# Loading k and q by head, turning them in program order, and holding six chunks at a change of batch

## The chip, the cores and the metric

The kernel runs on one core of a Trainium2 chip. Its time is the device time of one execution in microseconds (us); lower is better. Three executions of the kernel before took 1262.25, 1262.31 and 1267.04 us, so the median is 1262.31 us. Engines are named as in the profile: PE is the matrix engine (PEld its weight loads), DVE the vector engine, ACT the scalar engine, POOL is GpSimd, SP the engine whose queue issues nearly all transfers (SPq).

## The reference

All inputs are float32 or float64 (the mixer's weights); the output is float32. The shapes are 8 batches, 8 heads, 576 tokens, 64 channels a head, 128 features. With `phi` for the features:

```python
def phi(x):
    proj = einsum('bhsd,df->bhsf', x, w_phi)
    proj = proj - max(abs(proj), axis=-1, keepdims=True)
    return concatenate([exp(proj), exp(-proj)], axis=-1)
q_p, k_p = phi(q), phi(k)
kv  = einsum('bhsf,bhsd->bhfd', k_p, v)
z   = sum(k_p, axis=2)
x   = einsum('bhsf,bhfd->bhsd', q_p, kv) / (einsum('bhsf,bhf->bhs', q_p, z)[..., None] + 1e-6)
x   = x as (batch, token, 8 * 64)
u   = x + (xT @ U @ V)T           # xT: tokens last; U is 576 x 32, V is 32 x 576
out = u + max(u @ w_ch1, 0) @ w_ch2   # 512 -> 2048 -> 512
```

So there are two parts: linear attention for each pair of batch and head, and a mixer over the tokens and channels of each batch.

## The kernel before

**Tiles and stages.** Of a batch's 576 tokens 512 (SM) are worked on as four tiles of 128 (NT = 4), and the last 64 (ST, the tail) apart: tails of two batches share a tile `xt`, and the tails of all batches make up a ninth group of mixer rows. Attention goes by pairs of heads (class `Pair`), four pairs a batch, 32 in all. The mixer goes by groups of 512 rows (class `Mixer`): the 8 batches, and then the tails.

**A pair.** k and q of two heads are loaded into a tile `raw` (tag "raw", two buffers, so k and q of one pair at a time). From batch 2 on (`self.split`) they are loaded in blocks of 32 x 32 so that one DVE instruction, `nc.vector.transpose` (L321, the *turn*), makes them channel by token in place. Then ACT and DVE split them into a high and a low part `T` (L324, L325), PE projects them (`pk` L470, `pq` L496), and ACT, DVE and POOL (an all-reduce over partitions) make the features. `kt` and `kv` are the sums over the tokens of k's features with v; DVE adds them up in `kv` (L407, L408, L411). `xp` (L555) is the product of q's features with `kv`, which `normalize` (L534) divides into the batch's token tile `x`; `xpt` (L542) is the same for the tail, into `xt`.

**The token stage** (class `Tokens`, function `tokens`), at the end of each batch: `x` is split (`xs`, L633, L634), multiplied with U (`pp`, L647), then with V for each of the four tiles and the tail (`vp`, L663; below `vp_0` to `vp_4`), added to `x` (L664) and stored to memory (`u_dram<-x`, L665). From there 16 transfers bring it back in blocks (`y<-u_dram`, L691), DVE turns it (L697), and ACT and DVE split it into `uT_hi` and `uT_lo` (L249, L250).

**The mixer's chunks.** A group's work is 32 chunks of 12 matmuls: 16 `hidden` (`ph`, L705, then the relu into `h_hi` L710 and `h_lo` L711) and 16 `add` (`o`, L726, onto four banks `o_0` to `o_3`). The chunks of one batch are mixed between the steps of the next batch's attention: the list `todo`, emptied by `mix`, at the pace of `Pace`. At the end of a batch `mix(len(todo) - HELD)` leaves `HELD` chunks of the old group for the time until the new group's `uT` is there. After an old group's last chunk, `finish` adds its banks onto rows that were loaded again (`st`, L745) and stores them (L746); the group of tails adds them onto `x_tail` (L749) and stores that (L755), and this ends the kernel.

**What sets the order.** The code is written in program order, but a scheduler orders each engine's instructions by a model of their times before the program is built. An instruction on which `tc.keep_in_program_order` is called stays behind whatever the code traced last on its engine. At run time each engine works in its built order, and a wait of one instruction holds all behind it on that engine. `keep_busy` adds small matmuls (`busy`) where no chunks are to be had.

## Time and profile before

| what | value |
|---|---|
| median of 3 runs | 1262.31 us (1262.25 to 1267.04) |
| profiled execution | 1269.13 us, its span 1267.3 us |
| mean granted clock of PE | 0.956 |
| PE, PEld busy | 1216.5 us (96%), 1032.7 us (81%) |
| DVE, ACT, POOL busy | 865.7, 622.1, 315.5 us |
| chain that ended last | 69% PE, 14% DVE, 5% SPq, 5% ACT |

The profile is of one execution. Its page gives busy times, a strip of 40 slices of the span with busy tenths and the clock that PE was granted, and the costliest groups of instructions. Matmuls are pipelined, so a busy PE is not a PE at its best: how many matmuls a stretch holds and the granted clock say more. Views by stretch give each engine's busy time and the clock between two points of time; timelines give single instructions with the idle time before them and what ended it.

### The profile page before, as it was taken

The page shows a single profiled execution, that of the slowest core. Times are in us where ns is not written, and L with a number is a line of the kernel's source. Part 1 is how long each engine was busy: PE and PEld are TensorE (multiplying, and loading weights), DVE is VectorE, ACT ScalarE, POOL GpSimd, SP SyncE. Part 2 cuts the span into 40 slices and gives each one's busy share as a digit, 9 for nine tenths or more (in the row PEclk, how much of TensorE's full clock was granted, in tenths as well). Part 3 has the DMA queues.
Part 4 walks back from the last instruction along what each step waited for, and adds up shares of the span by engine and source line. Part 5 has one row for each costly group of instructions (what it writes and reads, how often), then busy time and mean ns, then how long its engine had stood idle before and what let it go on. Part 6 is the DMA issues. An engine that isn't in the chain of part 4 may idle for free.

```text
span 1267.3 us, 18400 instructions
## 1 busy us (share of the span) xinstructions
PE 1216.5 (96%) x6331; PEld 1032.7 (81%) x6333; DVE 865.7 (68%) x1781; ACT 622.1 (49%) x1271; POOL 315.5 (25%) x202
## 2 busy tenths in 40 slices
PE   8999998999997999999999999899998999999997
PEld 7878887878886888888887888688887888788886
DVE  5857879877789767888789868876788663412211
ACT  6857687535554555555555455444555541111110
POOL 3433434321322213223232323132223230000000
PEclk9979998989996999989998999889998999999999
DMA  4767222332326332453336223633245114811311
GB/s 134 244 232 239 72 70 62 86 91 75 77 71 150 79 78 63 135 117 76 82 103 146 65 74 83 150 84 79 62 117 129 42 51 139 197 67 50 100 67 33
DMA packets 268893, 129.03 MB, mean 102 GB/s; under 512 B 228944, under 2 KB 241536, under 8 KB 268800
## 3 DMA queue, kind: packets, MB, share of 16 engines
q1 hardware_dynamic: 268800, 127.86, 37.1%
q8 instruction: 50, 0.82, 0.3%
q14 instruction: 43, 0.35, 0.1%
HBM read 103.63 MB, written 24.17 MB: 101 GB/s over the span
## 4 chain that ended last, share of the span: by engine, by line
PE 69%; DVE 14%; SPq 5%; ACT 5%; DMA 4%; issue 3%; POOL 1%; DVEq 0%; ACTq 0%; POOLq 0%
PE ph L705 25%; PE o L726 25%; PE xp L555 7%; PE kt L387 3%; SPq L271 2%; SPq L691 2%; DVE T L325 2%; PE pk L470 2%; DVE w L242 2%; DMA y<-u_dram 1%; PE pp L647 1%; PE xpt L542 1%; DMA u_dram<-x 1%; ACT w_ab L138 1%; PE kv_ps L516 1%
## 5 line engine op out<-in xcount | busy, mean ns | idle before, releaser
L705 PE MATMUL ph<-uT_hi,w 128*128 128x512 f32 x1152 | 392.2, 401 | 1.9 <-DVE h_lo L711 1.2
L726 PE MATMUL o<-w,h_hi 128*128 128x512 f32 x1152 | 315.4, 398 | 3.8 <-ACT h_hi L710 3.6
L705 PEld LDWEIGHTS ph<-uT_hi,w 128*128 128x128 f32 x1152 | 221.0, 193 | 47.0 <-DVE h_lo L711 1.7
L726 PEld LDWEIGHTS o<-w,h_hi 128*128 128x128 f32 x1152 | 213.5, 190 | 49.3 <-ACT h_hi L710 6.7
L705 PE MATMUL ph<-uT_lo,w 128*128 128x512 f32 x576 | 230.3, 400 | 4.4 <-DVE uT_lo L250 4.3
L711 DVE SCALAR_TENSOR_TENSOR h_lo<-ph,h_hi 128x512 fp32r<-128x512 f32 x144 | 98.8, 687 | 171.8 <-ACT h_hi L710 170.6
L358 POOL PARTITION_ALL_REDUCE zs<-zs x48 | 106.6, 2221 | 414.0 <-DVE zs L357 373.6
L710 ACT ACTIVATE h_hi<-ph 128x512 fp32r<-128x512 f32 x144 | 85.9, 597 | 242.7 <-PE ph L705 231.6
L726 PE MATMUL o<-w,h_lo 128*128 128x512 f32 x576 | 183.6, 394 | 0.0
L434 POOL PARTITION_ALL_REDUCE qp<-qp x64 | 132.6, 2073 | 152.6 <-ACT qp L433 152.4
L555 PEld LDWEIGHTS xp<-kv,qp 128*128 128x128 f32 x1024 | 135.8, 210 | 4.8 <-ACT qp L436 0.7
L555 PE MATMUL xp<-kv,qp 128*128 128x65 f32 x1024 | 137.3, 292 | 0.5 <-DVE kp_t L421 0.3
L705 PEld LDWEIGHTS ph<-uT_lo,w 128*128 128x128 f32 x576 | 111.0, 193 | 29.8 <-DVE uT_lo L250 8.0
L726 PEld LDWEIGHTS o<-w,h_lo 128*128 128x128 f32 x576 | 105.3, 188 | 19.2
L325 DVE TENSOR_TENSOR T<-raw,T 64x512 fp32r<-64x512 f32 x96 | 77.0, 802 | 13.8 <-ACT T L324 11.0
L424 ACT ACTIVATE kp<-kp 128x512 f32<-128x512 f32 x64 | 40.5, 632 | 84.1 <-DVE kp L421 50.9
L436 ACT ACTIVATE qp<-qp 128x512 f32<-128x512 f32 x64 | 40.3, 630 | 53.3 <-DVE qp L435 52.9
L324 ACT CAST T<-raw 64x512 fp32r<-64x512 f32 x96 | 59.3, 618 | 14.5 <-PE pq L496 12.7
L146 POOL INT64_ADD w_ab<-w_ab x32 | 44.3, 1384 | 79.7 <-DVE w_ab L142 48.9
L372 DVE TENSOR_TENSOR klo<-kp,khi 128x1024 fp32r<-128x1024 f32 x48 | 60.9, 1268 | 2.5 <-PE kt L387 2.2
L473 ACT COPY kp<-pk 128x256 f32<-128x256 f32 x96 | 34.3, 371 | 52.4 <-PE pk L470 52.0
L321 DVE STREAM_TRANSPOSE raw<-raw 128x512 f32<-128x512 f32 x48 | 34.0, 709 | 37.9 <-DMA raw<-in_q_dram 21.0
(146 smaller groups left out, 1836.5 us busy)
## 6 DMA issues: line engine op xcount, KB each, us to landing
w<-kept SPq DMA_DIRECT2D x78, 512.0 KB
words<-in_moe_w_ch_dram SPq DMA_DIRECT2D x32, 512.0 KB
vb<-in_v_dram SPq DMA_DIRECT2D x64, 128.0 KB
u_dram<-x SPq DMA_DIRECT2D x32, 256.0 KB
st<-u_dram SPq DMA_DIRECT2D x16, 512.0 KB
out_dram<-st SPq DMA_DIRECT2D x32, 256.0 KB
y<-u_dram SPq DMA_DIRECT2D x112, 64.0 KB
raw<-in_k_dram SPq DMA_DIRECT2D x192, 32.0 KB
```

Of the source, the lines that this page charges most:

```text
L146: nc.gpsimd.int64_add(a64, a64, b64)
L324: nc.scalar.copy(out=m[here, s, :], in_=x_[here])
L325: nc.vector.tensor_sub(m[there, s, :], x_[here], f32(m[here, s, :]))
L358: nc.gpsimd.partition_all_reduce(zs[:, 1, :], zs[:, 0, :], P, ReduceOp.add)
L372: nc.vector.tensor_sub(lo, kp, f32(hi))
L424: nc.scalar.activation(out=kp[:, :, 0:F], in_=kp[:, :, F:2 * F], func=AF.Exp)
L434: nc.gpsimd.partition_all_reduce(qp[:, 0, :], qp[:, 1, :], P, ReduceOp.absmax)
L555: nc.tensor.matmul(xv[:, c, :], qp[:, f, c * P:(c + 1) * P], self.kv[:, f, c // 2 if self.split else s, :], start=(f == 0), stop=(f == 1))
L705: nc.tensor.matmul(ph, w1_part(f, l, c), r[:, c, :], start=(n == 0), stop=(n == 3 * NCC - 1))
L710: on_act = nc.scalar.activation(out=h_hi, in_=ph, func=AF.Relu)
L711: on_dve = nc.vector.scalar_tensor_tensor(out=h_lo, in0=ph, scalar=0.0, in1=f32(h_hi), op0=ALU.max, op1=ALU.subtract)
L726: nc.tensor.matmul(self.o[t], l[:, cs], w2_t[f][:, r, :], start=(f == 0 and n == 0), stop=(f == NFC - 1 and n == 2))
```

## The change

1. From batch 2 on, `raw` of k and of q is loaded by 4 transfers (one for each head and half of the channels, all 512 tokens) instead of 8. A head's 512 tokens now stand on the 64 partitions of that head, where before each half of the tokens stood on 64 partitions for both heads. So `T[n][:, s, :]` is head s where it was half s; `project_k_split`, `out_main` and `normalize` follow, and the branches for the old layout go.
2. The turn is kept in program order on DVE.
3. `HELD` is 6 where it was 4. Between the ends of batches 32 - HELD chunks are paced.
4. The memset of `xt`'s second half for later pairs of batches is on GpSimd.
5. The last group's last chunk is kept in program order on PE, and each of its four banks is stored by itself, half its rows over SP's queue and half over ACT's.

The line numbers of the changed kernel are 2 to 10 lower than those named here from L277 on.

```diff
@@ Pair.__init__
                 if self.split:
+                    to = m.rearrange("p h (j r) -> p (h j) r", r=Q)
                     for i in range(4):
-                        rs = slice(i // 2 * (SM // 2), (i // 2 + 1) * (SM // 2))
                         cs = slice(i % 2 * Q, (i % 2 + 1) * Q)
-                        for g in range(2):
-                            self.loaded = nc.sync.dma_start(
-                                out=m[i * Q:(i + 1) * Q, g, :].rearrange(
-                                    "c (j r) -> c j r", r=Q),
-                                in_=src[b, self.h0 + g, rs, cs].rearrange(
-                                    "(j c) r -> c j r", c=Q))
+                        self.loaded = nc.sync.dma_start(
+                            out=to[i * Q:(i + 1) * Q],
+                            in_=src[b, self.h0 + i // 2, 0:SM, cs].rearrange(
+                                "(j c) r -> c j r", c=Q))
@@ Pair.transposes
-                    nc.vector.transpose(out=x_, in_=x_)
+                    tc.keep_in_program_order(nc.vector.transpose(out=x_, in_=x_))
@@ Pair.project_k_split
                 for i in range(2):
-                    cs = slice((2 * g + s) * P, (2 * g + s + 1) * P)
+                    cs = slice((2 * s + i) * P, (2 * s + i + 1) * P)
                     nc.tensor.matmul(
-                        pk[:, i, :, :], self.T[0][:, i, cs], w_hl, start=True, stop=True)
-                ts_ = slice(s, NT, 2)
+                        pk[:, i, :, :], self.T[0][:, g, cs], w_hl, start=True, stop=True)
+                ts_ = slice(2 * s, 2 * s + 2)
@@ Pair.normalize
-            num, db = xv[:, :, 0:D], den.unsqueeze(2).broadcast_to([np_, m, D])
-            if len(xo.shape) == 4:
-                num, db = (a.rearrange("p (g z) d -> p g z d", g=2) for a in (num, db))
-            nc.vector.tensor_tensor(out=xo, in0=num, in1=db, op=ALU.mult)
+            nc.vector.tensor_tensor(
+                out=xo, in0=xv[:, :, 0:D], in1=den.unsqueeze(2).broadcast_to([np_, m, D]),
+                op=ALU.mult)
@@ Pair.out_main
-                        self.kv[:, f, c // 2 if self.split else s, :],
-                        start=(f == 0), stop=(f == 1))
-            if not self.split:
-                h = self.h0 + s
-                self.normalize(s, xv, x[:, :, h * D:(h + 1) * D])
-                return
-            xo = x.rearrange("p (s z) c -> p s z c", s=2)[:, s, :, self.h0 * D:(self.h0 + 2) * D]
-            self.normalize(s, xv, xo.rearrange("p z (g d) -> p g z d", g=2))
+                        self.kv[:, f, s, :], start=(f == 0), stop=(f == 1))
+            h = self.h0 + s
+            self.normalize(s, xv, x[:, :, h * D:(h + 1) * D])
@@ Mixer.add
-                    nc.tensor.matmul(
+                    ins = nc.tensor.matmul(
                         self.o[t], l[:, cs], w2_t[f][:, r, :],
                         start=(f == 0 and n == 0), stop=(f == NFC - 1 and n == 2))
+                    if self.g == B and f == NFC - 1:
+                        tc.keep_in_program_order(ins)
@@ Mixer.finish
                 nc.vector.tensor_add(self.x[:, t, :], self.x[:, t, :], self.o[t])
-                if t % 2 == 1:
-
-                    tails = out[2 * t - 2:2 * t + 2, SM:S, :].rearrange(
-                        "(t s) r e -> s r t e", s=2)
-                    for s in range(2):
-                        nc.sync.dma_start(
-                            out=tails[s], in_=self.x[s * ST:(s + 1) * ST, t - 1:t + 1, :])
+                for s in range(2):
+                    (nc.sync, nc.scalar)[s].dma_start(
+                        out=out[2 * t + s, SM:S, :], in_=self.x[s * ST:(s + 1) * ST, t, :])
@@
-    HELD = 4
+    HELD = 6
@@
-                        nc.vector.memset(xt[ST:P], 0.0)
+                        nc.gpsimd.memset(xt[ST:P], 0.0)
```

All five points change the built order. Three places of it follow.

On PE at the end of batch 4, the piece that ends with the last full token tile's `vp_3`, before (`ph_15`, `o`: chunks of the old group, hence chunk matmuls):

```order
L705 MATMUL ph_15_6876<-uT_hi_5331,w_2410 128x512
L705 MATMUL ph_15_6876<-uT_lo_5332,w_2410 128x512
L705 MATMUL ph_15_6876<-uT_hi_5331,w_2410 128x512 x2
L705 MATMUL ph_15_6876<-uT_lo_5332,w_2410 128x512
L705 MATMUL ph_15_6876<-uT_hi_5331,w_2410 128x512 x2
L705 MATMUL ph_15_6876<-uT_lo_5332,w_2410 128x512
L705 MATMUL ph_15_6876<-uT_hi_5331,w_2410 128x512 x2
L705 MATMUL ph_15_6876<-uT_lo_5332,w_2410 128x512
L705 MATMUL ph_15_6876<-uT_hi_5331,w_2410 128x512
L726 MATMUL o_0_5734<-w_14_2325,h_lo_14_6845 128x512
L726 MATMUL o_1_5735<-w_14_2325,h_lo_14_6845 128x512
L663 MATMUL vp_3_6750<-pst_6000,v_all 128x512
```

and now, from `vp_0` on:

```order
L655 MATMUL vp_0_6564<-pst_5856,v_all 128x512
L655 MATMUL vp_1_6568<-pst_5856,v_all 128x512
L655 MATMUL vp_2_6572<-pst_5856,v_all 128x512
L718 MATMUL o_0_5738<-w_2365,h_hi_15_6891 128x512 x2
L718 MATMUL o_1_5739<-w_2365,h_hi_15_6891 128x512 x2
L718 MATMUL o_2_5740<-w_2365,h_hi_15_6891 128x512 x2
L718 MATMUL o_3_5741<-w_2365,h_hi_15_6891 128x512 x2
L655 MATMUL vp_3_6576<-pst_5856,v_all 128x512
```

Before, 22 chunk matmuls stood between `vp_2` and `vp_3` (the 14 of these rows, and eight of `o` ahead of them), and 14 more from there up to the new group's first `ph`. Now it is 8 and 4; the other chunks of the old group stand ahead of `vp_0`.

On DVE at the end of batch 3, before (`raw_2_1` is q of the third pair of the next batch, `xt` the tile of tails):

```order
L664 TENSOR_TENSOR x_4049<-x_4049,vp_2_5323 128x512
L435 TENSOR_TENSOR qp_0_1_5286<-qp_0_1_5286 128x512
L321 STREAM_TRANSPOSE raw_2_1_5491<-raw_2_1_5491 128x512
L664 TENSOR_TENSOR x_4049<-x_4049,vp_3_5327 128x512
L711 SCALAR_TENSOR_TENSOR h_lo_15_5467<-ph_15_5453,h_hi_15_5466 128x512
L664 TENSOR_TENSOR xt_2626<-xt_2626,vp_4_5390 64x512
L394 TENSOR_TENSOR kvT_0_5280<-kt_4_0_5362,kvT_0_5280 64x256
L379 TENSOR_TENSOR v_hl_1_5603<-vb_97,v_hl_1_5603 128x8x64
L407 COPY kv_0_5478<-kv_ps_0_5475 128x260
L967 MEMSET xt_5470 64x512
```

and now:

```order
L656 TENSOR_TENSOR x_3968<-x_3968,vp_2_5181 128x512
L656 TENSOR_TENSOR x_3968<-x_3968,vp_3_5185 128x512
L433 TENSOR_TENSOR qp_0_1_5146<-qp_0_1_5146 128x512
L703 SCALAR_TENSOR_TENSOR h_lo_15_5503<-ph_15_5489,h_hi_15_5502 128x512
L656 TENSOR_TENSOR xt_2577<-xt_2577,vp_4_5250 64x512
L392 TENSOR_TENSOR kvT_0_5140<-kt_4_0_5222,kvT_0_5140 64x256
L405 COPY kv_0_5365<-kv_ps_0_5362 128x260
L377 TENSOR_TENSOR v_hl_1_5486<-vb_97,v_hl_1_5486 128x8x64
L409 TENSOR_TENSOR kv_0_5365<-kv_0_5365,zc_0_5129 128x4
L689 STREAM_TRANSPOSE y_5191<-y_5191 128x512
```

The turn and the memset are gone from this place; the turn of that pair now stands behind the new batch's first features.

On PE at the kernel's end, before:

```order
L726 MATMUL o_0_11557<-w_2410,h_hi_15_11977 128x512 x2
L726 MATMUL o_1_11558<-w_2410,h_hi_15_11977 128x512 x2
L726 MATMUL o_2_11559<-w_2410,h_hi_15_11977 128x512 x2
L726 MATMUL o_3_11560<-w_2410,h_hi_15_11977 128x512 x2
L726 MATMUL o_0_11557<-w_2410,h_lo_15_11978 128x512
L726 MATMUL o_1_11558<-w_2410,h_lo_15_11978 128x512
L726 MATMUL o_2_11559<-w_2410,h_lo_15_11978 128x512
L726 MATMUL o_3_11560<-w_2410,h_lo_15_11978 128x512
```

and now:

```order
L718 MATMUL o_0_11365<-w_2365,h_hi_15_11785 128x512 x2
L718 MATMUL o_0_11365<-w_2365,h_lo_15_11786 128x512
L718 MATMUL o_1_11366<-w_2365,h_hi_15_11785 128x512 x2
L718 MATMUL o_1_11366<-w_2365,h_lo_15_11786 128x512
L718 MATMUL o_2_11367<-w_2365,h_hi_15_11785 128x512 x2
L718 MATMUL o_2_11367<-w_2365,h_lo_15_11786 128x512
L718 MATMUL o_3_11368<-w_2365,h_hi_15_11785 128x512 x2
L718 MATMUL o_3_11368<-w_2365,h_lo_15_11786 128x512
```

Each bank is now complete three matmuls after the one before it, where all four were completed by the last four.

## The prediction

> **What bounds the kernel now.** I read the page first, then the profile cut into stretches, then the waits and the timelines at the places where the stretches differ. The page:
>
> ```profile
> span 1267.3 us, 18400 instructions
> PE 1216.5 (96%) x6331; PEld 1032.7 (81%) x6333; DVE 865.7 (68%) x1781; ACT 622.1 (49%) x1271; POOL 315.5 (25%) x202
> PEclk9979998989996999989998999889998999999999
> ```
>
> PE is busy all the time, and its granted clock dips at regular places. The next rows cut the span there. Columns: stretch in us, its length, then PE, PEld, DVE, ACT and POOL busy us with instructions, granted clock, DMA share, GB/s.
>
> ```profile
> 380.00:420.00 40.00, 32.45 (x135) 25.91 (x134) 35.97 (x73) 21.43 (x44) 11.44 (x7) 0.70 0.58 143
> 430.00:470.00 40.00, 40.00 (x220) 34.46 (x219) 28.17 (x61) 20.64 (x44) 9.20 (x5) 1.00 0.29 70
> 525.00:550.00 25.00, 21.77 (x99) 18.90 (x98) 20.27 (x45) 8.79 (x18) 0.06 (x1) 0.80 0.65 154
> 660.00:685.00 25.00, 22.29 (x102) 18.12 (x100) 20.26 (x46) 10.81 (x22) 0.58 (x2) 0.86 0.64 153
> 801.00:835.00 34.00, 29.27 (x119) 24.10 (x118) 29.14 (x60) 14.69 (x32) 6.93 (x4) 0.70 0.59 138
> 943.00:967.00 24.00, 20.64 (x96) 16.57 (x94) 21.92 (x47) 11.20 (x23) 3.19 (x2) 0.79 0.68 161
> 1063.00:1090.00 27.00, 25.52 (x112) 20.40 (x111) 11.67 (x19) 4.46 (x8) 0.00 (x0) 1.00 0.70 199
> 1100.00:1140.00 40.00, 40.00 (x178) 33.09 (x177) 7.46 (x11) 4.19 (x7) 0.00 (x0) 1.00 0.31 91
> ```
>
> Away from the changes of batch (430 and 1100) PE has no idle time and the full clock: nothing can be won there without fewer matmuls, and the two programs' orders hold the same 5524 PE instructions. The other six rows are the ends of batches 2 to 7. What such an end costs I count as PE's idle time plus the clock that was not granted: (1 - 0.70) x 40 + 7.55 = 19.6 us for batch 2, then 5.0 + 3.2 = 8.2, 3.5 + 2.7 = 6.2, 10.2 + 4.7 = 14.9, 5.0 + 3.4 = 8.4, and 1.5 us for batch 7. Their sum, 58.8 us, is all that the ends of batches can give.
>
> Why PE runs dry there is read from the timelines, batch 3 first (start, us, engine, line; idle time before in brackets):
>
> ```profile
> 525.14 0.84 PE L663 MATMUL vp<-pst,v_all 128*128 128x512 f32 x3
> 530.81 0.39 PE L663 MATMUL vp<-pst,v_all 128*128 128x512 f32 x1
> 531.12 0.71 DVE L321 STREAM_TRANSPOSE raw<-raw 128x512 f32<-128x512 f32 x1 [2.97 <-DMA raw<-in_q_dram]
> 531.75 0.65 DVE L664 TENSOR_TENSOR x<-x,vp 128x512 f32<-128x512 f32 x1
> 534.51 8.37 SPq L691 DMA_DIRECT2D y<-u_dram  x16
> 539.91 0.80 PE L470 MATMUL pk<-w_hl,T 128*128 128x256 f32 x2 [3.23 <-DVE kv L408]
> ```
>
> The last full token tile's `vp` stands 5.7 us behind the first three, its add follows at 531.75, the tile goes to memory, and only then do the 16 loads of `y` begin, which the queue takes 8.37 us to issue (0.52 each). Until `y` has come and been turned, no first-layer matmul of the batch can run. PE lives on what stands between `vp_0` and the new batch's first `ph`: chunks of the old batch and the next pair's attention. When that is used up it stops, and the clock falls. So an end of batch is worth (chain from `vp_0` to `y`) minus (cover on PE behind `vp_0`).
>
> **The change part by part.** *Six chunks held.* A chunk is 12 matmuls:
>
> ```profile
> 1110.15 2.72 PE ph L705 x12
> ```
>
> that is 0.227 us each at the full clock, and two more would be 5.4 us of cover, over the idle time of any end but batch 2's. But the built order, not the number held, says what stands behind `vp_0`. Counting chunk matmuls from `vp_0` to the first new `ph`, before and changed: batch 2 0 and 0, batch 3 36 and 36, batch 4 36 and 12, batch 5 12 and 12, batch 6 12 and 12, batch 7 72 and 50. The rest of what is held has been drawn ahead of `vp_0`, where PE is full anyway. The second count that matters is the chunk matmuls ahead of the last `vp_3`, since the chain starts there: 22 to 8 in batches 3 and 4, 8 to 8 in 5, 8 to 12 in 6, 22 to 10 in 7. Hence, in idle us:
> - batch 2: 0, its order on PE has the same cover.
> - batch 3: chain shorter by 14 x 0.227 = 3.2, same cover: -3.2.
> - batch 4: chain -3.2, cover 24 x 0.227 = 5.4 less: +2.2.
> - batch 5: 0.
> - batch 6: `vp_3`'s add now stands on DVE behind the four adds of the old batch's result; four such adds are 2.48 us in the row of the kernel's end below: +2.5.
> - batch 7: chain 12 x 0.227 = 2.7 shorter, cover 22 x 0.227 = 5.0 less: +2.3.
>
> *Turns in program order.* The queue's and DVE's waits:
>
> ```profile
> DVE raw L321 <- DMA raw<-in_q_dram: 21.0, 11, 3.0
> DVE raw L321 <- DMA raw<-in_k_dram: 9.1, 10, 1.5
> SPq L271 <- DVE T L325: 96.6, 38, 13.8
> ```
>
> DVE stood 30.1 us for loads it was made to turn early; the turn now comes where its data has long landed, one pair's worth of work later. Where that fell in a stretch like 430 to 470, PE was full: worth 0. In batches 3 and 4 such a wait stands right ahead of `vp_3`'s add. In batch 3 the turn ends at 531.8 and `vp_3` at 531.2, so 0.6 us of the 2.97 reached the chain; I take 0.5 for each of the two: -1.0. If the turn were late, the next pair's `T` would be, and PE's `pk`; a pair's work hides that.
>
> *Four loads instead of eight.* 384 transfers of 32 KB become 192 of 64 KB, the size of a `y` load. Rows:
>
> ```profile
> 524.87 3.29 SPq L271 DMA_DIRECT2D raw<-in_q_dram  x7
> 528.25 0.39 SPq L665 DMA_DIRECT2D u_dram<-x  x1
> ```
>
> 0.47 us a piece, so 8 x 0.47 = 3.8 us of queue become 4 x 0.52 = 2.1. What waits behind them on SP is `u_dram<-x`, the first of which went at 528.25. But the chain hangs on `vp_3`'s tile, added by 532.4, by when the loads are out: 0, and at most -1.7 at two ends.
>
> *Memset on GpSimd.*
>
> ```profile
> L967 DVE MEMSET xt<- 64x512 f32 x3 | 1.5, 485 | 1.1 <-DMA u_dram<-xt 0.9 <-issue 0.2
> L315 POOL MEMSET tail_T<- 128x256 f32 x8 | 2.7, 331 | 21.7 <-PE pqt L487 19.8 <-ACT qp L433 1.9
> ```
>
> DVE loses 3 x 0.485 and 1.1 us of waiting, -2.6 us at best. POOL has the nearest price, 0.33 us, and is a quarter busy. But the wait moves with it: at batch 3 the store of `xt` now stands behind the 16 `y` loads, 8.37 us later, and behind the waiting memset stand all-reduces for `zs` and `qp_t` that the next pair needs, while DVE's `xt` product waits for it; +2 at worst. I take 0, as both ends lie in a place with its own idle time.
>
> *By head.* The projections have as many matmuls and copies (L470, L473, L474); the product in `normalize` keeps 128x256 elements with one dimension less. All four tiles of a pair are now final only after its second head, so the split of two tiles waits longer before `pp`. In batches 3 to 5, 24 chunk matmuls (5.4 us) stand between the pair's last product and `pp`, against 21 before, which hides it; in batch 6 only 16. I take 0, at most +0.5 an end, one more split on DVE:
>
> ```profile
> L634 DVE TENSOR_TENSOR xs<-x,xs 128x256 fp32r<-128x256 f32 x64 | 27.9, 463 | 4.6 <-ACT xs L633 4.5
> ```
>
>
> *The end by bank.*
>
> ```profile
> 1258.68 1.07 PE L726 MATMUL o<-w,h_lo 128*128 128x512 f32 x4
> 1259.11 2.48 DVE L749 TENSOR_TENSOR x_tail<-x_tail,o 128x512 f32<-128x512 f32 x4 [3.44 <-PE o L726]
> L755 SPq DMA_DIRECT2D out_dram<-x_tail x4: 621/674/1025, 1260.4 to 1262.5; - x4
> ```
>
> The last matmul ends at 1259.75, the four adds at 1261.59, and the last issue starts at 1262.5, so it is out some 3.8 us after the last matmul. Bank by bank, three adds fall under the matmuls; the last ends 0.68 after, and one issue on each of two queues (0.62) follows: 1.3. That is -2.5 if issuing sets the end. If the 1 MB of writes does, the first issue counts: 1260.4 was 0.65 after the last matmul, and would be 2.04 - 0.68 = 1.36 ahead of it: -2.0. I take -2.2.
>
> *The sum.* Ends of batches 3 to 6: -3.2 + 2.2 + 2.5 - 1.0 = +0.5 us of idle time. With each idle us there went 23.7 / 14.0 = 1.7 us of clock not granted (sums over the rows of batches 3 to 6), so +0.5 x 2.7 = +1.4. Batch 7 +2.3, the end -2.2: **+1.5 us**. The profiled execution took 1269.13 us, 1.8 outside its span, and is 6.8 above the median of the three runs, 1262.31; the sum is a difference and goes on the median: **1264 us**, no change.
>
> **The clock.** Rows:
>
> ```profile
> 673.88 0.51 PE L470 MATMUL pk<-w_hl,T 128*128 128x256 f32 x2 [1.95 <-DVE kv L408]
> 671.00:684.00 13.00, 10.58 (x46) 8.48 (x44) 11.91 (x30) 6.69 (x14) 0.00 (x0) 0.74 0.76 162
> 1083.29 2.12 PE L726 MATMUL o<-w,h_hi 128*128 128x512 f32 x8 [1.48 <-ACT h_hi L710]
> ```
>
> One idle piece of 1.95 us at batch 4 was followed by a clock of 0.74 over 13 us; 1.48 us at batch 7 left it at 1.00. So the point from which the clock is taken seems to lie between 1.5 and 2.0 us in one piece. The Trainium skill (TensorE: Matmul & The Clock Gate, Part 1) has the clock halved after an idle window of about 3.4 us. By that rule batch 4 would have kept its clock, and the added idle time here would cost itself alone: +0.5 + 2.3 - 2.2, 1263 us. The trace does not agree, and decides.
>
> **The rivals.** *S, slower: the clock is lost at three ends.* Place: batches 4, 6 and 7, where idle time is added. Batch 7 stands at 1.48 us and would have 3.8, over the point of 2.0. If batches 4 and 6 then cost what batch 5 does now (14.9) and batch 7 what batch 3 does (8.2): +8.7 + 6.5 + 6.7, less 3.2 + 1.0 + 2.2 elsewhere: +15.5, 1278 us. For it: batch 5 has the very cover (12) that 4 gets. Against it: batch 6 has that cover too and costs 8.4.
>
> *F, faster: the ends get cheap.* Without the early turns and with shorter queues on SP and DVE, the chain shortens by more than the orders tell, and idle pieces fall under 2 us. Batch 3 goes to 0 (-8.2), batch 5 to batch 6's price (-6.5), batch 6 to batch 4's (-2.2), batch 4 stays, and the end gives -2.2: -19.1, 1243 us. For it: in batch 5 PE stood twice, and between the two a turn stood on DVE ahead of the `kv` (L408) for which PE waited; in the changed order it is gone from there:
>
> ```profile
> 808.56 0.47 PE L444 MATMUL pkt<-w_hl,tail_T 128*128 128x128 f32 x1 [1.96 <-DVE xt L664]
> 810.06 0.70 DVE L321 STREAM_TRANSPOSE raw<-raw 128x512 f32<-128x512 f32 x1
> 811.39 0.80 PE L470 MATMUL pk<-w_hl,T 128*128 128x256 f32 x2 [1.12 <-DVE kv L408]
> ```
>
>  Against it: the 16 `y` issues, 8.37 us, stay in every chain.
>
> *T: nothing moves at the ends of batches* since what is held is drawn forward anyway, and only the kernel's end gains: 1260 us.
>
> **How the numbers follow.** This measurement can tell about 0.5% from no change: 1256.0 to 1268.6. The forecast has 0.40, T 0.06, S 0.26 and F 0.28. Spread about the forecast (1256 to 1269 is its own range) gives 0.02 more to faster and takes 0.01 from slower: faster 0.30, the same 0.45, slower 0.25. The range reaches to both rivals, cut a little short of each: 1246 to 1277.
>
> **What would show it.** Right: clock 1.00 and PE without idle time mid-batch; no wait of DVE's turn for `raw`; the end after the last matmul 2 us shorter; batch 3 cheaper, batches 4, 6 and 7 dearer in idle time plus clock not granted. S: a clock under 1.00 in batch 7's stretch. F: ends of batches 3 to 6 together under 20 us against 37.7 now. Wrong in its root: if held chunks stand as I counted, and PE's idle time still shrinks, then the chain was set by DVE's or SP's queue and not by where `vp_3` stands.

## The result, and the profile after

Eight executions of each kernel were timed on one chip. The changed kernel took 1273.4 us in the median (1267.9 to 1275.5), the kernel before 1263.7 us (1258.1 to 1267.0). The ratio is 1.0070, with a 95% interval of 1.0046 to 1.0094: the change made the kernel slower by 0.7%, some 9.7 us. The forecast was no change at 1264 us. The time lies within the range of 1246 to 1277, on the side that was given 0.25, and outside the spread of 1256 to 1269 that the prediction gave to its own forecast.

The page of the changed kernel; its profiled execution took 1271.15 us:

```profile
span 1269.4 us, 18096 instructions
PEclk9979999999996999999997999899997999999999
```

The ends of batches 2 to 7, each in one stretch of 55 to 80 us, first of the kernel before and then of the changed one. Columns: stretch, length, busy us of PE, PEld, DVE, ACT and POOL with instructions, granted clock, DMA share, GB/s.

```profile
360.00:440.00 80.00, 72.45 (x356) 60.45 (x356) 66.73 (x140) 41.39 (x86) 20.09 (x11) 0.85 0.44 108
505.00:570.00 65.00, 61.77 (x323) 53.70 (x322) 55.45 (x110) 34.04 (x70) 18.92 (x10) 0.92 0.49 123
645.00:710.00 65.00, 62.13 (x324) 52.47 (x323) 56.34 (x110) 34.84 (x73) 16.22 (x9) 0.95 0.53 132
785.00:850.00 65.00, 60.27 (x283) 50.61 (x282) 54.62 (x105) 32.40 (x69) 16.64 (x9) 0.84 0.49 119
930.00:995.00 65.00, 60.17 (x301) 49.79 (x300) 56.63 (x117) 35.77 (x74) 19.02 (x10) 0.92 0.48 118
1055.00:1110.00 55.00, 53.52 (x241) 43.71 (x240) 21.23 (x35) 8.99 (x16) 0.00 (x0) 1.00 0.65 175
```

```profile
360.00:440.00 80.00, 73.92 (x372) 61.88 (x371) 66.64 (x141) 41.03 (x85) 21.34 (x12) 0.87 0.41 102
505.00:570.00 65.00, 60.53 (x320) 51.40 (x319) 54.47 (x111) 34.19 (x71) 16.00 (x9) 0.97 0.50 124
645.00:710.00 65.00, 58.63 (x282) 49.35 (x281) 52.11 (x103) 34.16 (x70) 18.34 (x9) 0.87 0.48 117
785.00:850.00 65.00, 57.48 (x273) 48.86 (x272) 48.00 (x99) 31.56 (x66) 15.46 (x10) 0.87 0.50 119
930.00:995.00 65.00, 57.60 (x295) 48.18 (x294) 54.65 (x114) 34.33 (x71) 19.72 (x10) 0.89 0.45 112
1055.00:1110.00 55.00, 52.45 (x251) 43.38 (x250) 23.14 (x47) 9.65 (x19) 0.00 (x0) 1.00 0.65 162
```

As in the prediction, the price of an end is PE's idle time plus the clock not granted (batch 4 after: 6.37 + 0.13 x 65 = 14.8). The forecast column has the terms of the prediction in the same unit, idle time times 2.7 for batches 3 to 6, with 0.5 us of DVE's early turn taken off in batches 3 and 4.

| end of batch | before | after | difference | forecast |
|---|---|---|---|---|
| 2 | 19.5 | 16.5 | -3.1 | 0 |
| 3 | 8.4 | 6.4 | -2.0 | -10.0 |
| 4 | 6.1 | 14.8 | +8.7 | +4.6 |
| 5 | 15.1 | 16.0 | +0.8 | 0 |
| 6 | 10.0 | 14.5 | +4.5 | +6.7 |
| 7 | 1.5 | 2.5 | +1.1 | +2.3 |
| behind the last matmul | 7.6 | 5.2 | -2.4 | -2.2 |
| sum | | | +7.7 | +1.5 |

The two profiled executions differ by only 2.0 us (1271.15 to 1269.13), since that of the kernel before was itself 5.5 us over its median. It lost 36.5 us in its first 360 us, where the changed kernel's lost 28.5, and that hides what the ends added. The sum of the table, +7.7, is near the +9.7 of the medians.

A price comes from one execution, and another execution of the same order can have another. The kernel before with only its end changed (an experiment below) has the same order on PE at these six ends; its prices are 19.7, 8.5, 5.9, 10.6, 8.9 and 2.3. Up to 0.2 us lies between the two at batches 2 to 4, but 4.5 at batch 5 and about 1 at batches 6 and 7. Against that execution the six ends sum to +14.9 us and not to the +10.1 of the table, so its nearness to the medians proves little.

What a dear end looks like: the end of batch 4 on DVE, then on PE (start, us, engine, line; idle time before in brackets):

```profile
661.31 0.68 DVE L739 TENSOR_TENSOR st<-st,o 128x512 f32<-128x512 f32 x1
...
662.47 1.88 DVE L739 TENSOR_TENSOR st<-st,o 128x512 f32<-128x512 f32 x3
...
664.87 0.67 DVE L656 TENSOR_TENSOR xt<-xt,vp 64x512 f32<-64x512 f32 x1
```

```profile
665.60 0.33 PE L442 MATMUL pkt<-w_hl,tail_T 128*128 128x128 f32 x1 [2.67 <-DVE xt L656]
...
669.21 1.21 PE L539 MATMUL xpt<-kv,qp_t 128*128 128x130 f32 x4 [2.25 <-DVE kp_t L419]
...
679.41 0.50 PE L468 MATMUL pk<-w_hl,T 128*128 128x256 f32 x2 [1.15 <-DVE kp L472]
```

The last `vp` ended at 662.2, but its add began only at 664.87, behind the four adds of the old group's result (`st`, 2.56 us) and other work. PE had no chunk of the old group left in its order and stood three times. The second stop is for `kp_t`, which stood on DVE behind a turn of `y` that itself waited 1.50 us for its load. Before, the four adds stood behind the token stage's adds, though still ahead of the `kv` add (L408) for which PE then stood 1.95 us, and 24 more chunk matmuls stood on PE.

### The profile page after: what moved, and what is told of

Same layout as the page of the kernel before. It is cut to its first block, busy times and chain, and to the rows that moved or that the text cites. A ratio compares the mean times of both kernels' runs of the same rounds, so it can differ in the third digit from the quotient of the medians.

```text
span 1269.4 us, 18096 instructions
## 1 busy us (share of the span) xinstructions
PE 1212.1 (95%) x6331; PEld 1029.7 (81%) x6333; DVE 860.3 (68%) x1778; ACT 619.1 (49%) x1271; POOL 318.6 (25%) x205
## 4 chain that ended last, share of the span: by engine, by line
PE 66%; DVE 12%; DMA 3%; ACT 2%; SPq 2%; issue 1%; POOL 0%; DVEq 0%; ACTq 0%; POOLq 0%
PE o L718 25%; PE ph L697 25%; PE xp L552 6%; PE kt L385 3%; SPq L683 2%; DMA u_dram<-x 1%; DVE T L323 1%; PE pk L468 1%; PE pp L639 1%; DMA y<-u_dram 1%; DVE uT_lo L250 1%; PE pq L493 1%; PE pq L494 1%; PE xpt L539 1%; DVE klo L370 1%
## 5 line engine op out<-in xcount | busy, mean ns | idle before, releaser
L356 POOL PARTITION_ALL_REDUCE zs<-zs x48 | 109.5, 2282 | 325.5 <-DVE zs L355 214.6
L718 PE MATMUL o<-w,h_lo 128*128 128x512 f32 x576 | 187.1, 394 | 0.0
L323 DVE TENSOR_TENSOR T<-raw,T 64x512 fp32r<-64x512 f32 x96 | 73.8, 768 | 13.2 <-ACT T L322 10.5
L369 ACT CAST khi<-kp 128x1024 fp32r<-128x1024 f32 x48 | 50.4, 1050 | 0.7
```

Source lines behind the costliest of these rows:

```text
L323: nc.vector.tensor_sub(m[there, s, :], x_[here], f32(m[here, s, :]))
L356: nc.gpsimd.partition_all_reduce(zs[:, 1, :], zs[:, 0, :], P, ReduceOp.add)
L369: nc.scalar.copy(out=hi, in_=kp)
L718: ins = nc.tensor.matmul(self.o[t], l[:, cs], w2_t[f][:, r, :], start=(f == 0 and n == 0), stop=(f == NFC - 1 and n == 2))
```

## The experiments

Each kernel was timed beside the kernel before on the same chip. Times are medians; the ratio is to the kernel before, with its 95% interval. "Cover" is the number of chunk matmuls from `vp_0` to the first new `ph` in the built order. Prices are in us, from stretches as above.

**Four held, else as changed.**

```diff
-    HELD = 6
+    HELD = 4
```

> The changed kernel with HELD back at 4, all else as changed. In its built order the chunk matmuls from vp_0 to the first new ph are 36 at each of batches 3 to 6 and 72 at batch 7, against 36, 12, 12, 12, 50 in the changed kernel. Theory A (an end of batch costs what the cover behind vp_0 leaves open, and six held chunks gave it away): batches 4, 5 and 6 fall from 14.8, 16.0 and 14.6 us of idle time and clock not granted to what 36 cost in the kernel before, 6 to 8 us, and batch 7 loses 1: some 23 us in all, 1273 to about 1250, 1% faster than before. Theory B (the memset on GpSimd and the store of xt behind it delay DVE's xt) and theory C (the pinned turn, or the layout by head) keep their cause here: both 1270 to 1274.

1257.9 us, ratio 0.9956 (0.9937 to 0.9975). The ends of batches 4 to 6:

```profile
645.00:710.00 65.00, 60.99 (x317) 50.52 (x316) 55.33 (x113) 34.78 (x73) 17.89 (x9) 0.97 0.51 127
785.00:850.00 65.00, 61.16 (x310) 50.85 (x310) 52.26 (x106) 31.34 (x63) 15.94 (x9) 0.95 0.48 122
930.00:995.00 65.00, 60.68 (x314) 51.44 (x313) 52.90 (x110) 31.75 (x67) 17.18 (x10) 0.95 0.41 102
```

They are 6.0, 7.1 and 7.6, as theory A had it; batch 3 rose to 11.7 with the same cover of 36, nearly all of it clock (0.97 to 0.89; idle time 4.47 and 4.53 us). 15.5 us came back of the 23 expected.

**The memset back on DVE.**

```diff
-                        nc.gpsimd.memset(xt[ST:P], 0.0)
+                        nc.vector.memset(xt[ST:P], 0.0)
```

> The changed kernel with the memset of xt back on DVE. Built order: 36, 12, 36, 12, 38 chunk matmuls behind vp_0 in batches 3 to 7, so batch 5 gets the cover that batch 4 lacks. Theory A: batch 5 falls from 16.0 us to 6 to 8, batch 7 rises by up to 2: about 1266. Theory B: all ends come back to the kernel before, whatever the cover: about 1261 (the end by bank stays), and batch 4 is cheap again in spite of 12. Theory C: 1272 to 1274.

1261.1 us, 0.9983 (0.9964 to 1.0001). The total is theory B's, the ends are theory A's: batch 4, with a cover of 12, stayed at 14.6; batch 5, now with 36, fell from 16.0 to 5.5; batch 7 rose from 2.5 to 7.3. So the memset seems to act by what it moves in the order. POOL's wait for the store of `xt`, which the move brought, was there in the changed kernel:

```profile
POOL xt L957 <- DMA u_dram<-xt: 49.6, 3, 17.6
```

That is three waits, 49.6 us together, and no sign of them in the price of batch 4.

**The turn free to move.**

```diff
-                    tc.keep_in_program_order(nc.vector.transpose(out=x_, in_=x_))
+                    nc.vector.transpose(out=x_, in_=x_)
```

> The changed kernel with the turn of raw free to move in the built order. Built order: 36, 36, 12, 12, 72 chunk matmuls behind vp_0 in batches 3 to 7, as in the kernel before. Theory A: batch 4 falls from 14.8 to 6 to 8 us, batch 7 loses 1, the rest as changed: about 1265, and DVE waits again some 20 to 30 us for raw without that showing. Theory B: no change, 1272 to 1274. Theory C (the pin delays what follows on DVE): about 1261, with batches 5 and 6 cheaper as well.

1262.1 us, 0.9983 (0.9965 to 1.0001). Batch 4 (cover 36) fell to 8.9; batches 5 and 6 (cover 12) stayed at 13.2 and 14.0. DVE waited 27.1 us for `raw` again, and the ends go with A. The total lies nearer to C, since the first 360 us lost 22.0 where the changed kernel lost 28.5, which no theory had.

**The end by bank alone, on the kernel before.**

```diff
+                    if self.g == B and f == NFC - 1:
+                        tc.keep_in_program_order(ins)
...
-                if t % 2 == 1:
+                for s in range(2):
+                    (nc.sync, nc.scalar)[s].dma_start(
+                        out=out[2 * t + s, SM:S, :], in_=self.x[s * ST:(s + 1) * ST, t, :])
```

> The kernel before with the last group's end by bank alone; its order is otherwise as before, with the same chunk matmuls at every end of batch. All theories: 2.0 to 2.5 us less after the last matmul, so 0.2% faster than before, 1261.4. If the 1 MB of writes set the end and not its issues, under 2.

1258.0 us, 0.9971 (0.9951 to 0.9991), so 1.1 to 6.2 us less. From the last matmul's end to the end of the span went 7.6 us before and 5.1 here.

**Batch 4 alone: held chunks pinned.** The first matmul of each chunk held at the end of batch 4 is kept in program order on PE (the same in `add`).

```diff
+                    if n == 0 and self.g in pinned:
+                        tc.keep_in_program_order(ins)
...
             mix(len(todo) - HELD)
+            if b == 4:
+                pinned.update(fn.__self__.g for fn, _ in todo)
```

> The changed kernel, six held, with one edit: at the end of batch 4 alone the first matmul of each held chunk of the old group is kept in program order on PE, behind what the token stage has traced. Built order behind vp_0: 36, 30, 36, 12, 50 chunk matmuls in batches 3 to 7, against 36, 12, 12, 12, 50; vp_3 at batch 4 has no chunk ahead of it. Theory A (the cover behind vp_0 sets the price of an end): prices so far, idle time and clock not granted in 65 us, were 5.5 to 11.7 us at 36 and 10 to 16 at 12, so batches 4 and 5 fall from 14.8 and 16.0 to 6 to 9 each, batches 6 and 7 stay: about 1273 - 15 = 1258. Theory Q (the chain is set by the queues of DVE, SP and POOL, and the counts only go along with it): batches 4 and 5 keep 13 to 16, 1270 to 1274.

1261.1 us, 0.9979 (0.9954 to 1.0004). Batch 5, where the cover came to 36 unpinned, fell to 5.2; batch 4, pinned, only to 12.6. Pinned chunks stand behind the next pair's `pk`, which waits for DVE (2.90 us there), and PE can't reach past it.

**All held chunks pinned, six held.**

```diff
             mix(len(todo) - HELD)
+            pinned.update(fn.__self__.g for fn, _ in todo)
```

> The changed kernel, six held, with the held chunks of every old group kept in program order in the same way. Built order: 30, 39, 39, 39, 39, 62 chunk matmuls behind vp_0 in batches 2 to 7, against 0, 36, 12, 12, 12, 50. Theory A: batch 2 falls from 16.5 us to 8 to 10, batches 4 to 6 from 45.3 together to some 20: 1273 - 33 = about 1240, 1.8% faster than before. Theory Q: 1268 to 1274.

1257.9 us, 0.9958 (0.9936 to 0.9980). Batches 4 to 6 fell to 8.6, 6.7 and 7.1, but batch 2 went to 20.0 in spite of its cover of 30, and batch 7 to 6.7. Half of the expected gain.

**Eight and seven held, pinned.**

```diff
-    HELD = 6
+    HELD = 8
```

> As the run with all held chunks pinned, but eight held. Built order: 51, 81, 81, 81, 81, 120 chunk matmuls behind vp_0 in batches 2 to 7, so the cover is over the chain from vp_0 to y (14 to 16 us: 81 x 0.227 = 18.4). Theory A: every end of batches 2 to 6 falls to 2 to 5 us, 1273 - 50 = about 1224, if the stretches between the ends stay full with 24 chunks paced instead of 26. Rival M (the stretches between run dry, since DVE's attention work sets their pace then): idle time there of 3 to 5 us a batch, about 1240, no better than six held. Theory Q: 1265 or over.

1273.4 us, 1.0068 (1.0044 to 1.0092). Theory A fails here: with a cover of 81 the ends of batches 2 to 6 cost 25.9, 18.0, 12.2, 16.9 and 9.9. Batch 3 on DVE, then on PE:

```profile
522.54 0.71 DVE L690 STREAM_TRANSPOSE y<-y 128x512 f32<-128x512 f32 x1 [3.34 <-DMA y<-u_dram]
...
523.35 0.41 DVE L407 TENSOR_TENSOR kv<-kv,kt 128x256 f32<-128x256 f32 x1
```

```profile
523.82 0.80 PE L469 MATMUL pk<-w_hl,T 128*128 128x256 f32 x2 [3.90 <-DVE kv L407]
```

A turn of `y` stood on DVE ahead of a `kv` that was ready, and waited 3.34 us for its load. PE stood 3.90 us at `pk` with the held chunks behind it.

> As the run with all held chunks pinned, but seven held. Built order: 51, 60, 60, 60, 60, 72 chunk matmuls behind vp_0 in batches 2 to 7, and on DVE the first turn of y stands behind kv and kp, where with eight held it stood ahead of kv. Theory Q (DVE's order sets the price: eight held lost because kv waited behind a turn of y that waited for its load): batches 3 to 6 cost 5 to 8 us each as with six pinned, no 12 to 18, and the time is within 5 us of that run's 1258. Theory A (cover counts as well): 3 to 5 each, and batch 2 falls from 20.0 to about 10: about 1237. Theory M (cover over some 40 chunk matmuls is of no use, because 25 paced chunks don't fill the rest): as eight held, 1268 or over.

1268.5 us, 1.0032 (1.0016 to 1.0048). Here no turn of `y` stood ahead of `kv`, and the time was still 10.6 us over that with six. Batches 4 to 6 cost 10.5 to 10.7, batch 3 16.4, and the stretch behind batch 3's end ran dry:

```profile
540.00:560.00 20.00, 16.27 (x79) 12.66 (x78) 16.71 (x27) 13.53 (x26) 5.90 (x3) 1.00 0.32 94
```

That is 3.7 us of idle time 28 to 48 us behind `vp_0`, with DVE busy 84%. The bound that theory Q gave (within 5 us) failed, and A with it. More chunks ahead only put PE's stops later, which is nearest to M.

**Six held, alone on the kernel before.**

```diff
-    HELD = 4
+    HELD = 6
```

> The kernel before with HELD 6 alone. Built order: 12, 60, 12, 36, 12, 74 chunk matmuls behind vp_0 in batches 2 to 7, against 0, 36, 36, 12, 12, 72 before. Theory A: batch 2 -4, batch 3 -4, batch 4 +7, batch 5 -6, batches 6 and 7 as before: 1264 - 7 = about 1257. Theory H (that six are held is itself what cost the 10 us, whatever the order): about 1274.

1269.0 us, 1.0046 (1.0021 to 1.0072). A had the sign at batches 2 to 5, not the sizes: batch 2 -5.7, 3 -1.3, 4 +10.8, 5 -3.9, and batch 6, expected unchanged, +4.4. The sum of the ends, with +0.2 at batch 7, is +4.5, and the ratio gives +5.8: nearer to H than to A. At batch 6 all 12 chunk matmuls stood ahead of `vp_3`, and the four `st` adds ahead of its add, as at batch 6 of the changed kernel.

**The four adds of an old group kept behind.**

```diff
-                    nc.vector.tensor_add(st, st, self.o[t])
+                    tc.keep_in_program_order(nc.vector.tensor_add(st, st, self.o[t]))
```

> The changed kernel, six held, with one edit: the four adds that end an old group (st) are kept in program order on DVE, so that they stand behind the token stage's adds and the next pair's kv and kp, where the changed kernel has them ahead at batches 4, 5 and 6. Built order: 84, 12, 12, 36, 12 chunk matmuls behind vp_0 in batches 2 to 6, so batches 4 and 6 keep the cover of 12 and batch 3 falls from 36 to 12. Theory A (cover alone sets the price): batches 4 and 6 keep 13 to 16 us, batch 3 rises from 6.4 to 10 to 16, batch 5 falls from 16.0 to 6 to 8, batch 2 falls from 16.5 to under 6: about 1258. Theory S (the price at 12 was that of the four adds, 2.5 us on DVE in the chain, which stand there whenever the old group ends early): batches 4, 5 and 6 all fall to 6 to 9, batch 3 stays at 6 to 9 in spite of 12: 1273 - 24, and up to 10 less for batch 2: 1240 to 1249.

1269.1 us, 1.0036 (1.0017 to 1.0055).

```profile
0.00:360.00 360.00, 333.95 (x1883) 286.00 (x1884) 283.04 (x597) 234.19 (x479) 133.08 (x105) 0.94 0.42 122
360.00:440.00 80.00, 77.31 (x404) 65.61 (x404) 61.40 (x123) 37.81 (x79) 17.38 (x9) 0.98 0.46 116
505.00:570.00 65.00, 59.95 (x285) 49.96 (x285) 55.05 (x110) 34.33 (x73) 17.17 (x11) 0.84 0.49 119
645.00:710.00 65.00, 57.08 (x303) 47.77 (x303) 56.15 (x116) 36.66 (x77) 18.30 (x10) 0.95 0.50 119
930.00:995.00 65.00, 57.78 (x305) 48.41 (x304) 56.24 (x119) 35.49 (x74) 18.57 (x10) 0.95 0.47 115
```

Batch 3, whose cover fell from 36 to 12, rose from 6.4 to 15.4 with no `st` add in the way, where theory S had 6 to 9. But its idle time rose only from 4.5 to 5.1 us; the rest is clock (0.97 to 0.84), which one execution doesn't settle. Batches 4 and 6, still at 12, fell to 11.2 and 10.5, under what A allowed, and the total is over both theories. Batch 2, with 84, fell from 16.5 to 4.3. In the profiled execution nearly all that the ends gained was given back in the first 360 us, 47.7 against 28.5 in the changed kernel.

**Eight loads instead of four.**

```diff
-                        self.loaded = nc.sync.dma_start(
-                            out=to[i * Q:(i + 1) * Q],
-                            in_=src[b, self.h0 + i // 2, 0:SM, cs].rearrange(
-                                "(j c) r -> c j r", c=Q))
+                        for u in range(2):
+                            self.loaded = nc.sync.dma_start(
+                                out=to[i * Q:(i + 1) * Q, u * 8:(u + 1) * 8],
+                                in_=src[b, self.h0 + i // 2, u * 256:(u + 1) * 256, cs].rearrange(
+                                    "(j c) r -> c j r", c=Q))
```

> The changed kernel, by head, with k and q loaded by 8 transfers of 32 KB again instead of 4 of 64 KB. Built order: the same chunk matmuls behind vp_0 in batches 2 to 5 and the adds of the old group at the same places on DVE in batches 2 to 5; batch 6 has its adds where batch 5 has them. All theories: the issues alone are worth -1.7 to +1.7 us at two ends, so 1271 to 1276. If the larger number of issues delays the stores of u_dram, batches 4 and 5 cost 1 to 3 us more: 1276 to 1279.

1256.5 us, 0.9936 (0.9914 to 0.9957): 17 us less than the changed kernel, where every theory had no change, and the fastest kernel of all. Batches 4, 5 and 6 cost 10.8, 9.7 and 9.5, with the same counts at 4 and 5. PE's second and third long stop at batch 5, changed kernel and then this one:

```profile
812.63 1.21 PE L539 MATMUL xpt<-kv,qp_t 128*128 128x130 f32 x4 [2.15 <-DVE kp_t L419]
824.41 0.67 PE L697 MATMUL ph<-uT_lo,w 128*128 128x512 f32 x1 [2.53 <-DVE uT_lo L250]
```

```profile
800.70 1.20 PE L540 MATMUL xpt<-kv,qp_t 128*128 128x130 f32 x4 [1.03 <-DVE kp_t L420]
810.50 0.51 PE L698 MATMUL ph<-uT_lo,w 128*128 128x512 f32 x1 [0.54 <-DVE uT_lo L250]
```

The first stop, for `xt`, is 2.80 us in both; the second is 1.12 us shorter and the third 1.99. Either the transfers or what stands elsewhere in the order did that, and the next run was to tell them apart.

**Eight loads, with all six held chunks pinned,** so that the orders with four and with eight loads are nearly one.

> The changed kernel with all six held chunks pinned (which took 1258) and with k and q loaded by 8 transfers of 32 KB instead of 4 of 64 KB. With 8 loads alone the changed kernel came to 1256.5, 17 us less, but there some 10% of the rows of PE's order and 17% of DVE's stand elsewhere too. Here the two orders are nearest to each other: 30, 39, 39, 39, 39, 62 chunk matmuls behind vp_0 in both, and 2 to 3% of PE's rows elsewhere. Theory T (the 64 KB transfers themselves cost the time, at run time: what stands behind them, u_dram and y, lands later): 10 to 17 us less, 1241 to 1248, 1.2 to 1.8% faster than before. Theory O (the number of transfers moves the built order, and the order moved the time): within 5 us of 1258.

1267.4 us, 1.0013 (0.9993 to 1.0032), against 0.9958 with four loads: eight loads were dearer here, by some 7 us going by the two ratios (0.0055 x 1264). Theory T falls by its sign, and O's bound is passed on the other side. SP's queue at batch 3, four loads and then eight:

```profile
516.92 1.93 SPq L271 DMA_DIRECT2D raw<-in_q_dram  x4
518.95 2.37 SPq L658 DMA_DIRECT2D u_dram<-x  x4
...
523.41 8.35 SPq L684 DMA_DIRECT2D y<-u_dram  x16
```

```profile
514.73 3.41 SPq L272 DMA_DIRECT2D raw<-in_q_dram  x7
518.24 1.36 SPq L659 DMA_DIRECT2D u_dram<-x  x3
...
522.97 8.45 SPq L685 DMA_DIRECT2D y<-u_dram  x16
```

`vp_0` was at 517.1 and at 514.8, so `y` was issued 6.3 us behind it with four loads and 8.2 with eight. The seven issues of `raw` held up `u_dram<-x`, and that held up `y`. Batches 3 to 6 cost 28.8 us together with four loads and 38.3 with eight. But their idle time is the same, 22.9 and 22.8 us: the 9.5 us between the prices are clock, and that the later `y` caused them is not shown.

## Why the prediction was right or wrong

**The total: near by luck.** The forecast was 9.4 us too low, and rival S's 1278 came nearer. The signs that the prediction named for itself did come: batch 3 cheaper, batches 4, 6 and 7 dearer, no idle time mid-batch, a shorter end. But the terms of its sum did not. At the ends of batches 3 to 6 it had +0.5 us of idle time; the rows show +10.1 (15.7 before, 25.8 after). It let 1.7 us of clock go with each idle us; the rows show some 2 us for all of the 10.1 (24.1 before, 26.0 after). At its own rate of 2.7 the measured idle time would have cost 27 us. The two errors hid each other. The rate was taken from one execution whose clock was poor: the kernel before with only its end changed lost 16.9 us of clock at these ends, where the kernel before lost 24.1.

**What bounds the kernel: right.** Away from the ends, 440 to 505, 570 to 645, 710 to 785 and 850 to 930, PE had no idle time and the clock was 1.00 in both kernels.

**Six chunks, counted in the order: right in sign, about half in size.** Over all kernels, the 18 ends of batches 3 to 6 that have a cover of 36 and no pinned chunks cost 5.2 to 11.7 us, 6.8 in the median, and the 20 with 12 cost 8.9 to 16.9, 13.1 in the median. Much of the 6.3 us between them is clock; in idle time alone the medians are 3.6 and 5.9. Where the same eight chunk matmuls stand ahead of `vp_3`, eight ends with a cover of 36 stand for 2.9 us in the median and sixteen with 12 for 5.6. These 2.7 us are half of what the prediction reckoned for 24 chunk matmuls, 5.4 at the full clock. Not all of it is shown to be the cover's: at most ends with 12 the `st` adds come early as well. The run that kept them behind had 0.6 us more idle time at batch 3, where the cover fell, and prices 3.6 and 4.0 less at batches 4 and 6, where eight loads had 4.0 and 5.0 less with the adds in the way. Batch 4 is the case the prediction named, +8.7 where it had +4.6, with +3.5 us of idle time where it had +1.7. Rival S had batches 4 and 6 lose their clock; batch 4 did so (0.95 to 0.87) and reached batch 5's price as S said, batch 6 rose by 4.5 and not 6.5, and batch 7 kept its clock.

**The step that failed is batch 3:** "chain shorter by 14 x 0.227 = 3.2, same cover: -3.2", with the clock -10.0. The chain did get shorter: `y` was issued 6.7 us behind `vp_0` and before 9.4. But PE's stop before was not that chain's. PE stood 3.23 us for the `kv` add (L408), which belongs to the next pair's attention and not to `y`. On DVE that add stood behind the memset and the four `st` adds:

```profile
536.26 0.48 DVE L967 MEMSET xt<- 64x512 f32 x1 [0.68 <-DMA u_dram<-xt]
536.77 1.28 DVE L745 TENSOR_TENSOR st<-st,o 128x512 f32<-128x512 f32 x2
...
538.05 1.28 DVE L745 TENSOR_TENSOR st<-st,o 128x512 f32<-128x512 f32 x2
...
539.45 0.41 DVE L408 TENSOR_TENSOR kv<-kv,kt 128x256 f32<-128x256 f32 x1
```

The first turn of `y` followed at 540.11 and did not wait for its load. In the changed kernel the same four adds stand ahead of `uT_lo`. On DVE

```profile
527.26 0.71 DVE L689 STREAM_TRANSPOSE y<-y 128x512 f32<-128x512 f32 x1 [0.41 <-DMA y<-u_dram]
527.90 2.44 DVE L739 TENSOR_TENSOR st<-st,o 128x512 f32<-128x512 f32 x4
...
530.47 0.67 DVE L250 TENSOR_TENSOR uT_lo<-y,uT_hi 128x512 fp32r<-128x512 f32 x1
```

and on PE

```profile
531.19 0.80 PE L697 MATMUL ph<-uT_lo,w 128*128 128x512 f32 x1 [2.02 <-DVE uT_lo L250]
```

The turned `y` lay for 2.44 us while DVE did the four `st` adds ahead of its `uT_lo`, and PE stood 2.02 us for that `uT_lo`. The idle time rose from 3.2 to 4.5 us, and only the clock got better (0.92 to 0.97). The prediction took the chain minus the cover, and left out DVE's own order between the two: a chain shorter by 2.7 us could not take 3.2 us off a stop that hung on those adds. The place of `vp_3` was worth less elsewhere too. Of the ends with a cover of 36, the ten with 22 or 23 chunk matmuls ahead of `vp_3` stand for 3.9 us in the median and the eight with 8 for 2.9, so 1.0 us lies between them and not 3.2. Of the 6.2 us between the forecast and the table (7.7 - 1.5) this term makes 8.0 and batch 4 another 4.1; batches 2, 6 and 7 gave 6.5 back.

**Batch 6, the `st` adds ahead of `vp_3`'s add: right,** +2.6 us of idle time for +2.5, and +4.5 for +6.7 with the clock. **Batch 5: right by luck only,** +0.8 for 0. Its idle time rose by 2.8 us; the price hardly moved because the clock of the execution before was low there (0.84, and 0.92 in the second execution of that order, against which batch 5 rose by 5.4). **Batch 7:** +1.1 for +2.3, at a clock of 1.00, and not as forecast. One stop is as long as the only one before, though for another tile (1.52 us for `uT_hi`, 1.48 for `h_hi` before). What came on top is a wait for a load of weights that the prediction doesn't have:

```profile
1105.92 0.50 PE L697 MATMUL ph<-uT_hi,w 128*128 128x512 f32 x1 [1.03 <-DMA w<-kept]
```

**The end by bank: right.** -2.4 for -2.2. The last rows of the changed kernel:

```profile
1262.17 2.73 DVE L743 TENSOR_TENSOR x_tail<-x_tail,o 128x512 f32<-128x512 f32 x4 [2.08 <-PE o L718]
1262.89 2.50 SPq L745 DMA_DIRECT2D out_dram<-x_tail  x4
1262.89 2.74 ACTq L745 DMA_DIRECT2D out_dram<-x_tail  x4
1263.78 0.39 PE L718 MATMUL o<-w,h_lo 128*128 128x512 f32 x1
```

Three of the four adds lie under the matmuls, and the first issues go out 1.3 us ahead of the last matmul's end.

**Turns, memset, loads.** DVE's wait for `raw` (30.1 us before) is gone from the list of waits, and nothing at the ends shows a gain from it. The loads were costed at 0, "at most -1.7 at two ends"; at an order held nearly fixed they took 1.9 us off the queue at batch 3's end and nothing off the idle time of the four ends. The run as a whole was some 7 us cheaper with four, and at these ends the gain is clock, for which the prediction has no term.

**What the prediction lacked as a whole** is that, save for the end by bank, no part of this change has a price of its own. Undone singly, four held gave back 15.5 us, the memset 12.3, the turn's pin 11.3 and the eight loads 17.0, which sums to 56 us for a change that cost 9.7. Each edit moves the built order at the ends, and as far as these runs show, the order that comes out decides. Six held is the one part that is dear both ways: put alone on the kernel before it cost 5.8 us, and taken back alone it gave 15.5. The layout by head was not undone alone, so its share is not shown. **Open** is why eight loads alone gave 17 us: some 10% of the rows of PE's order stand elsewhere (2 to 3% in the pair with pinned chunks), and the counts used here don't tell the two apart. Open too is why the kernel before and its variant with the end by bank lost 36.5 and 36.7 us in the first 360 us of their profiled executions, which took 5.5 and 6.9 us more than their medians. Their idle time there (18.5 and 18.7 us) is near the changed kernel's 17.7, so it is the clock: 0.95 in both against 0.97.

## What to carry to other kernels

Where a scheduler makes the order, undo each part of a change singly before crediting any part: the parts need not add. At a change of stage, count what the matrix engine has to do behind the start of the chain. Read first which instruction it waits for, then what the vector engine does ahead of that, and which instruction the cover stands behind: work behind a waiting instruction is no cover. In idle time, work held back was worth about half its own length here, and seven or eight pinned chunks made a slower kernel than six. Judge a stage by its idle time and its clock apart: the price of one end differed by 4.5 us between two executions of one and the same order, at nearly the same idle time.

## What the runs showed of the hardware

The prediction had the clock fall from a point between 1.5 and 2.0 us of idle time in one piece. The runs show no such point. One piece of the kernel before, and the clock around it:

```profile
194.03 1.95 PE L500 MATMUL pq<-T,w_two 128*128 128x256 f32 x4 [1.50 <-DVE x L534]
```

```profile
190.00:202.00 12.00, 10.50 (x59) 9.01 (x57) 10.30 (x17) 10.18 (x20) 5.67 (x4) 0.86 0.21 38
```

And one of the kernel with eight held, at the end of batch 7:

```profile
1079.64 0.50 PE L698 MATMUL ph<-uT_hi,w 128*128 128x512 f32 x1 [2.25 <-DVE h_lo L706]
```

```profile
1070.00:1090.00 20.00, 17.75 (x79) 14.38 (x78) 5.91 (x9) 3.06 (x6) 0.00 (x0) 1.00 0.75 184
```

1.50 us cost clock, 2.25 us cost none. The Trainium skill (TensorE: Matmul & The Clock Gate, Part 1) has the gate watch a free-running window of about 3.4 us. By that, where a piece falls in the window could matter and not its length alone, though neither piece here fills a window. What decides between the two rows no run here shows. The spread of the prices shows the same: with one and the same order at the end of batch 5, the kernel before lost 15.1 us there and its variant with the end by bank 10.6, in idle time that differs by 0.7 us (4.7 and 5.4) and a clock of 0.84 and 0.92.
